# Linear attention, two mixtures and a cosine layer on one core: the tail's keys' products move into each step's sum

## The chip, the cores and the metric

One core of a Trainium2 chip runs the whole kernel. The metric is device microseconds of one execution. In profiled executions the profile also gives the span from the first to the last instruction.

## The reference

Attention with random features (a linear attention) is followed by two dense parts. Cut to what the change touches:

```python
# q, k, v: (2 batches, 8 heads, 576 tokens, 64);  omega: (128 features, 64)
def phi(x):
    proj = np.einsum('bhsd,md->bhsm', x, omega)
    h = proj - np.sum(x * x, axis=-1, keepdims=True) / 2.0
    h = h - np.max(h, axis=-1, keepdims=True)
    return np.exp(h) / np.sqrt(m)
q_p, k_p = phi(q * scale), phi(k * scale)
kv = np.einsum('bhsm,bhsd->bhmd', k_p, v)      # the keys' products: a sum over all 576 tokens
z = np.sum(k_p, axis=2)
num = np.einsum('bhsm,bhmd->bhsd', q_p, kv)
den = np.einsum('bhsm,bhm->bhs', q_p, z)[..., None] + 1e-06
x = num / den                                  # -> (1152 tokens, 512)
# then four experts: out += p[:, e:e+1] * (relu(x @ w1[e]) @ w2[e])
# then h = out @ w_in; result = (h * cos(h)) @ w_out
```

All arithmetic of the attention is in 32-bit floats.

## The kernel before

The 576 tokens of a batch are cut into 512 and a tail of 64. The 512 are worked on in eight pieces, one for each batch `b` and each pair of heads `hp`; in a piece a token is `4 * partition + r`, so each head has four groups `r` of 128 tokens. The tails of both batches stand together in one tile of 128 partitions, batch 0 in partitions 0 to 63, batch 1 in 64 to 127: `kL`, `qL`, `veL` (values, with a column of ones that gives the sum `z`), and `phiL`, the features of the tail's keys for all eight heads.

The attention is a loop over steps `s`, written out by hand, which sets the order of every engine's work. In a step TensorE makes, in this order: the numerators of the piece before last (`nums`, at the end of the step before), the keys' products of the last piece (`kv_of`), transposes of the next queries and keys (`turn_ahead`: `tp_q`, `tp_k`), transposes of the queries' features (`turn_phi`: `tq`), projections (`features`: `pj_q`, `pj_k`) and a transpose of the finished piece (`put_x`: `tx`). From step 6 on some products of the first expert (`dense_quanta`: `g`) stand between. After the loop come the dense parts, in an order of their own. A step's other engines: VectorE takes maxima of the projections, shifts, copies and divisions; ScalarE takes the exponentials and some copies; GpSimd sums squares.

The keys' products are in `kv_of(i)`. For each of the piece's two heads and each `r` the helper `column_halves` makes two products, one for each half of the 128 features, so that each uses 64 columns of the TensorE array and all 128 rows; the two stand in different columns. They are summed in PSUM over `r`. As the program's names go, the tile that is written is `kv` in the first step, and in later steps a free stretch of the bank that the numerators `num` of head 1 use (`room`), so in the profile `num<-ve,phk` is the keys' products too, and `num<-kv,pT` the numerators.

The tail's keys' products are made once, in step 1, by `kv_tail`: for each head, each half of the features and each batch one product of 64 rows and 64 columns, so that four neighbours use the four quarters of the array. They go to four banks (`kvL_z_b`), which VectorE copies to the tile `kvL`. In every step `kv_of` ends with a VectorE addition of the sum in PSUM and the part of `kvL` that belongs to it.

Of the kernel before, what the change touches and what calls it, by code (L numbers as in the profile page):

```python
# [9 lines left out]
F32 = mybir.dt.float32  # L10
F32R = mybir.dt.float32r
U32 = mybir.dt.uint32
ACTF = mybir.ActivationFunctionType
ALU = mybir.AluOpType
# [12 lines left out]
def performer_moe_kernel(ctx, tc, q, k, v, omega, probs, w1, w2, w_in, w_out, out):  # L27
    nc = tc.nc
    B, H, S, D = q.shape
    M = omega.shape[0]  # L30
# [31 lines left out]
    def bank(name):  # L62
        return ps.tile([P, 512], F32, tag="ps", name=name)
# [886 lines left out]
    with tc.tile_pool(name="at1", bufs=1) as at1, tc.tile_pool(name="at2", bufs=2) as at2:  # L950
# [102 lines left out]
        def features(nm, turned, phi, squares=None, shift_later=False):  # L1053

            nb = at2.tile([P, 2 * R], F32, tag=f"nb{nm}"[:3], name=f"nb_{nm}")
            pjs = [bank(f"pj_{nm}_{g}") for g in range(2)]
            for i in range(R):
                c = slice(i * P, (i + 1) * P)
                for z, (x_, y) in enumerate([(turned, ws)] + [(squares, minus_norm)] * (squares is not None)):
                    for g, pj in enumerate(pjs):  # L1060
                        r = slice(g * D, (g + 1) * D)
                        nc.tensor.matmul(  # L1062
                            pj[:, i * M : (i + 1) * M], x_[r, c], y[r, :],
                            start=z == 0, stop=z == (squares is not None),
                        )
            yield
            three = at2.tile([P, 2 * R, 3], F32, tag=f"th{nm[0]}", name=f"three_{nm}")
            def square_sum():
                nc.vector.tensor_reduce(out=three[:, :, 1], in_=sqs.pop(nm), op=ALU.add, axis=AX.X)

            if squares is None and nm != "q0":
                square_sum()
            for g, pj in enumerate(pjs):
                to = (nb if squares is not None else three[:, :, 0])[:, g : 2 * R : 2]
                nc.vector.tensor_reduce(
                    out=to, in_=pj.rearrange("p (a m) -> p a m", m=M), op=ALU.max, axis=AX.X,
                    negate=squares is not None,
                )
            if shift_later:
                yield  # L1080
            if squares is None:
                if nm == "q0":
                    square_sum()
                nc.vector.tensor_reduce(
                    out=three[:, :, 2], in_=three[:, :, 0:2], op=ALU.add, axis=AX.X, negate=True
                )
                nc.vector.tensor_reduce(out=nb, in_=three[:, :, 1:3], op=ALU.add, axis=AX.X)
            yield
            for g, pj in enumerate(pjs):
                for i in range(4):  # L1090
                    ix = g + 2 * i
                    nc.scalar.activation(
                        phi[:, ix, :], pj[:, i * M : (i + 1) * M], ACTF.Exp, bias=nb[:, ix : ix + 1]
                    )
                yield

        def divide(nm, parts):

# [36 lines left out]
        xss, phks, phqs, kts, qts = {}, {}, {}, {}, {}  # L1135

        kv = [at1.tile([P, 2, B, D + 1], F32, name=f"kv{hp}") for hp in range(NP)]
        kvL = at1.tile([P, H, B, D + 1], F32, name="kvL")

        def column_halves(dst, weights, moving, start=True, stop=True):  # L1140
            for z in range(2):
                c = slice(z * P // 2, (z + 1) * P // 2)
                nc.tensor.matmul(dst[c], weights[:, c], moving, start=start, stop=stop)  # L1143

        def kv_tail(phi):
            for z in range(2):
                hs = range(z * H // 2, (z + 1) * H // 2)
                sums_ = [
                    bank(f"kvL_{z}_{b}")[:, : H // 2 * (D + 1)].rearrange("p (h e) -> p h e", e=D + 1) for b in range(B)
                ]  # L1150
                for n, h in enumerate(hs):
                    for c in (slice(0, P // 2), slice(P // 2, P)):
                        for b in range(B):
                            bl = slice(b * L, (b + 1) * L)
                            nc.tensor.matmul(
                                sums_[b][c, n, :], phi[bl, h, c], veL[bl, h, :], start=True, stop=True
                            )
                for b in range(B):
                    nc.vector.tensor_copy(out=kvL[:, hs.start : hs.stop, b, :], in_=sums_[b])

        def kv_of(i):
            b, hp = pairs[i]
            ve, phk = ves[i % 2], phks.pop(i)
            kvp = room.pop() if room else bank(f"kv_{i}")
            kvp = kvp[:, 4 * (D + 1) : 6 * (D + 1)].rearrange("p (h e) -> p h e", h=2)
            for h in range(2):
                for r in range(R):
                    column_halves(
                        kvp[:, h, :], phk[:, h * R + r, :], ve[:, h * R + r, :], r == 0, r == R - 1
                    )  # L1170
            yield
            nc.vector.tensor_tensor(out=kv[hp][:, :, b, :], in0=kvp, in1=kvL[:, 2 * hp : 2 * hp + 2, b, :], op=ALU.add)

        pTs = {}
        room = []
# [173 lines left out]
        for s in range(NPR + 3):  # L1349
            if s == 0:  # L1350
                load_k(3)
                load_q(2)
                load_v(1)
            else:
                if s == 1:
                    advance(wload)
                if s > NPR:
                    dense_quanta(s, 2 * DQ)
                kvs = kv_of(s - 1) if s <= NPR else iter(())
                next(kvs, None)  # L1360
                if s == 1:
                    turn_phi(0)
                    kv_tail(phiL)
                    next(kvs, None)
                else:
                    turn_ahead(s)
                    if s < first:
                        advance(wload)
                    for _ in ks:
                        pass  # L1370
                    next(ns, None)
                    next(kvs, None)
                if s >= first:
                    advance(wload)
                if 2 <= s <= NPR:
                    turn_phi(s - 1)
                elif s == NPR + 1:
                    tail_turn_phi()
                px = iter(())
                if 2 <= s <= NPR + 1:  # L1380
                    b, hp = pairs[s - 2]
                    px = put_x(f"{s - 2}", hp, xss.pop(s - 2), b * R, R)
                qs = q_features(s) if s <= NPR else iter(())
                ks = k_features(s + 1, s < first) if s + 1 < NPR else iter(())
                next(qs, None)
                next(ks, None)
                next(px, None)
                next(px, None)
                next(qs, None)
                next(ks, None)  # L1390
                for _ in px:
                    pass
                dense_quanta(s, (2 if s > NPR else 4) * DQ)
                for _ in qs:
                    pass
                if s + 1 <= NPR:
                    norms_ahead(f"q{s + 1}", q_of(s + 1))
                if s + 2 < NPR:
                    norms_ahead(f"k{s + 2}", kts[s + 2])
                if s <= NPR:  # L1400
                    ns = nums(s - 1)
                    next(ns)
                elif s == NPR + 1:
                    tail_nums()
                else:
                    for _ in tail_put_x():
                        pass
                if s + 3 < NPR:
                    load_k(s + 3)
                if s + 2 < NPR:  # L1410
                    load_q(s + 2)
                if s + 1 < NPR:
                    load_v(s + 1)
            advance(wload)
            for kind, u in fetched.get(s, ()):
                wload.append(load_a(0, u, "p") if kind == "p" else load_v2(0, u))
                next(wload[-1])
            if s == 2:
                nc.vector.tensor_reduce(out=psum_, in_=pr, op=ALU.add, axis=AX.X)
            if s == 4:  # L1420
                nc.scalar.activation(psum_, psum_, ACTF.Copy, bias=1e-9)
            if s == first:
                nc.vector.reciprocal(out=psum_, in_=psum_)
                nc.vector.tensor_tensor(
                    out=pn, in0=pr, in1=psum_.to_broadcast([P, NTILE, E]), op=ALU.mult
                )
# [39 lines left out]
```

## Time and profile before

| | us |
|---|---|
| median of 3 runs (640.3 to 640.7) | 640.69 |
| profiled execution | 640.93 |
| its span | 639.2 |
| TensorE busy | 633.7 (99% of the span) |
| VectorE busy | 488.5 (76%) |
| ScalarE busy | 352.8 (55%) |
| GpSimd busy | 173.8 (27%) |

TensorE's granted clock is 1.00, that is 2.4 GHz, over the span. A matmul's end is modelled in the profile, so that its busy time covers short waits; what TensorE really spends is read from the starts of successive rows. A product in 32-bit floats leaves two records, so sixteen products are `x32`; a transpose leaves one.

### The profile page before, as it was taken

Reading aid. Unit: us, or ns where it says so; the run is one execution under the profiler, and the core shown is the slowest. Engines: PE = TensorE matmul, PEld = TensorE weight load, DVE = VectorE, ACT = ScalarE, POOL = GpSimd, SP = SyncE. Lnnn points to the kernel's source line nnn. Section 1 sums busy time; section 2 is a strip of 40 time slices with the busy share of each in tenths; the row PEclk is TensorE's granted clock in tenths of the full one; section 3 lists DMA queues with packets and bytes.
Section 4 is the critical chain, followed back from the end, with each engine's and each line's share of the span. In section 5 each row is a group of like instructions: output and inputs, shape, how many; then the busy total and the mean of one; then the engine's idle time right before and its main releaser. Section 6 shows DMA issues by size and latency. Waiting matters only on the chain.

```text
span 639.2 us, 10046 instructions
## 1 busy us (share of the span) xinstructions
PE 633.7 (99%) x3751; PEld 538.0 (84%) x3751; DVE 488.5 (76%) x878; ACT 352.8 (55%) x686; POOL 173.8 (27%) x218
## 2 busy tenths in 40 slices
PE   8999999999999999999999999999999999999997
PEld 7999989988888888888888888888888888888887
DVE  5998578789688688598687697699698772697842
ACT  6898664365346454354443455544457973476821
POOL 7899752033332333323333232310000000000000
PEclk9999999999999999999999999999999999999999
DMA  7645430313446434347424445401250002500111
GB/s 166 188 118 149 133 100 31 102 67 131 133 148 200 146 106 143 128 148 217 134 98 132 138 130 209 132 35 70 85 208 33 2 0 91 239 1 2 49 50 49
DMA packets 55440, 70.95 MB, mean 111 GB/s; under 512 B 15200, under 2 KB 40032, under 8 KB 55392
## 3 DMA queue, kind: packets, MB, share of 16 engines
q1 hardware_dynamic: 46800, 40.92, 20.5%
q0 software_dynamic: 8448, 29.37, 13.5%
q8 instruction: 29, 0.48, 0.3%
q14 instruction: 19, 0.16, 0.1%
q10 hardware_dynamic: 144, 0.03, 0.0%
HBM read 55.36 MB, written 14.94 MB: 110 GB/s over the span
## 4 chain that ended last, share of the span: by engine, by line
PE 97%; DVE 1%; DMA 1%; SPq 0%; issue 0%; DVEq 0%
PE g L779 46%; PE g_odd L585 4%; PE g L549 3%; PE g_1c L549 2%; PE g_0a L549 2%; PE g_3a L549 2%; PE g_2a L549 2%; PE g_1a L549 2%; PE g_3c L549 2%; PE g_2c L549 2%; PE g_0c L549 2%; PE num L1143 2%; PE pj_q L1062 1%; PE g_0d L549 1%; PE g_0b L549 1%; PE g_3e L549 1%
## 5 line engine op out<-in xcount | busy, mean ns | idle before, releaser
L749 ACT ACTIVATE sth<-h 128x512 fp32r<-128x512 f32 (+1 forms) x111 | 60.3, 555 | 80.3 <-PE g L779 66.4
L258 POOL TENSOR_TENSOR c<-c 128x512 uint32<-128x512 uint32 x32 | 46.9, 1467 | 84.6 <-issue 34.2
L752 DVE SCALAR_TENSOR_TENSOR stl<-h,sth 128x512 fp32r<-128x512 f32 (+1 forms) x72 | 48.9, 694 | 27.1 <-ACT sth L749 26.9
L779 PE MATMUL g<-v3h,sth 128*128 128x512 f32 (+1 forms) x110 | 42.9, 390 | 0.0
L779 PE MATMUL g<-v0h,sth 128*128 128x512 f32 (+1 forms) x110 | 42.7, 388 | 0.0
L779 PE MATMUL g<-v1h,sth 128*128 128x512 f32 (+1 forms) x110 | 42.7, 388 | 0.0
L779 PE MATMUL g<-v2h,stl 128*128 128x512 f32 (+1 forms) x110 | 42.5, 387 | 0.0
L779 PE MATMUL g<-v2h,sth 128*128 128x512 f32 (+1 forms) x110 | 42.5, 386 | 0.0
L779 PE MATMUL g<-v0h,stl 128*128 128x512 f32 (+1 forms) x110 | 42.4, 386 | 0.0
L779 PE MATMUL g<-v3l,sth 128*128 128x512 f32 (+1 forms) x110 | 42.4, 386 | 0.0
L779 PE MATMUL g<-v3h,stl 128*128 128x512 f32 (+1 forms) x110 | 42.4, 386 | 0.0
L779 PE MATMUL g<-v1h,stl 128*128 128x512 f32 (+1 forms) x110 | 42.4, 385 | 0.0
L779 PE MATMUL g<-v1l,sth 128*128 128x512 f32 (+1 forms) x110 | 42.4, 385 | 0.0
L779 PE MATMUL g<-v0l,sth 128*128 128x512 f32 (+1 forms) x110 | 42.4, 385 | 0.0
L779 PE MATMUL g<-v2l,sth 128*128 128x512 f32 (+1 forms) x110 | 42.4, 385 | 0.0
L293 DVE TENSOR_TENSOR stl<-h,sth 128x512 fp32r<-128x512 f32 (+1 forms) x39 | 22.8, 594 | 19.3 <-ACT sth L749 19.1
L451 DVE SCALAR_TENSOR_TENSOR c<-c 128x512 f32<-128x512 f32 (+1 forms) x38 | 25.0, 662 | 11.9 <-ACT c L449 11.7
L448 ACT ACTIVATE c<-h 128x512 f32<-128x512 f32 x32 | 19.9, 621 | 19.8 <-DVE h L626 19.8
L805 DVE SCALAR_TENSOR_TENSOR acc<-g,pn,acc 128x512 f32<-128x512 f32 x27 | 20.1, 745 | 6.7 <-PE g L779 6.7
L779 PEld LDWEIGHTS g<-v2h,stl 128*128 128x128 f32 x110 | 20.7, 188 | 4.5 <-DVE stl L752 0.4
L779 PEld LDWEIGHTS g<-v0h,stl 128*128 128x128 f32 x110 | 20.7, 188 | 4.3 <-DVE stl L752 0.2
L779 PEld LDWEIGHTS g<-v3h,stl 128*128 128x128 f32 x110 | 20.7, 188 | 4.2
(427 smaller groups left out, 1880.5 us busy)
## 6 DMA issues: line engine op xcount, KB each, us to landing
rv<-in_moe_w_dram SPq DMA_DIRECT2D x16, 512.0 KB, 3.9
c<-in_moe_w_in_dram POOLq DMA_DIRECT2D x16, 512.0 KB, 4.1
c<-in_moe_w_out_dram POOLq DMA_DIRECT2D x16, 512.0 KB, 3.9
kt<-in_k_dram SPq DMA_DIRECT2D x8, 256.0 KB, 3.5
qt<-in_q_dram SPq DMA_DIRECT2D x8, 256.0 KB, 4.0
ve<-in_v_dram SPq DMA_DIRECT2D x16, 128.0 KB, 4.0
ra_2as<-in_moe_w_dram SPq DMA_DIRECT2D x8, 256.0 KB, 3.3
out_dram<-acc SPq DMA_DIRECT2D x7, 256.0 KB, 2.3
```

What stands on the lines that cost most here:

```text
L258: nc.gpsimd.tensor_tensor(out=total, in0=t, in1=lw, op=ALU.add)
L293: nc.vector.tensor_tensor(out=dst, in0=x, in1=y, op=ALU.subtract)
L448: nc.scalar.activation(vv, src, ACTF.Copy, bias=0.25, scale=INV_2PI)
L451: nc.vector.scalar_tensor_tensor(out=vv, in0=kk, scalar=ROUND, in1=vv, op0=ALU.subtract, op1=ALU.subtract)
L549: nc.tensor.matmul(dst, x[:, o], y[:, kk], start=start and n == 0, stop=stop and n == 3 * kn - 1, skip_group_check=reopen,)
L585: nc.tensor.matmul(g, x[:, kk], w[:, :, :, kk, :], start=n == 0, stop=n == 3 * KD - 1)
L749: nc.scalar.activation(hi, src, ACTF.Relu if self.e < E else ACTF.Copy)
L752: nc.vector.scalar_tensor_tensor(out=to, in0=src, scalar=0.0, in1=hi.bitcast(F32), op0=ALU.max, op1=ALU.subtract)
L779: nc.tensor.matmul(g, x, y[:, o : o + w], start=n == 0, stop=n == 3 * FT - 1)
L805: nc.vector.scalar_tensor_tensor(out=acc[t], in0=src, scalar=p_, in1=acc[t], op0=ALU.mult, op1=ALU.add)
L1062: nc.tensor.matmul(pj[:, i * M : (i + 1) * M], x_[r, c], y[r, :], start=z == 0, stop=z == (squares is not None),)
L1143: nc.tensor.matmul(dst[c], weights[:, c], moving, start=start, stop=stop)
```

## The change

`kv_tail`, its four banks, the tile `kvL` and the four copies go. In `kv_of` each head's sum gets one more pair of products behind its four: the two halves of the features again, from `phiL` and `veL`, in the 64 partitions of the piece's batch, so of 64 rows and 64 columns. The sum is stopped there, and VectorE's addition becomes a copy. Those are as many products of the tail as before (32), four in each of eight steps. In `features` the eight exponentials of the tail's keys come in the order of heads 0, 1, 2, 4, 6, 3, 5, 7 in place of 0, 2, 4, 6, 1, 3, 5, 7. The others keep their order; the generator loses yields behind the exponentials that no caller relied on.

```diff
-            for g, pj in enumerate(pjs):
-                for i in range(4):
-                    ix = g + 2 * i
-                    nc.scalar.activation(
-                        phi[:, ix, :], pj[:, i * M : (i + 1) * M], ACTF.Exp, bias=nb[:, ix : ix + 1]
-                    )
-                yield
+            order = [g + 2 * i for g in range(2) for i in range(R)]
+            if squares is not None:
+                order.insert(1, order.pop(R))
+            for ix in order:
+                i, g = divmod(ix, 2)
+                nc.scalar.activation(
+                    phi[:, ix, :], pjs[g][:, i * M : (i + 1) * M], ACTF.Exp, bias=nb[:, ix : ix + 1]
+                )
...
-        def kv_tail(phi):
-            for z in range(2):
-                hs = range(z * H // 2, (z + 1) * H // 2)
-                sums_ = [
-                    bank(f"kvL_{z}_{b}")[:, : H // 2 * (D + 1)].rearrange("p (h e) -> p h e", e=D + 1) for b in range(B)
-                ]
-                for n, h in enumerate(hs):
-                    for c in (slice(0, P // 2), slice(P // 2, P)):
-                        for b in range(B):
-                            bl = slice(b * L, (b + 1) * L)
-                            nc.tensor.matmul(
-                                sums_[b][c, n, :], phi[bl, h, c], veL[bl, h, :], start=True, stop=True
-                            )
-                for b in range(B):
-                    nc.vector.tensor_copy(out=kvL[:, hs.start : hs.stop, b, :], in_=sums_[b])
...
+            bl = slice(b * L, (b + 1) * L)
             for h in range(2):
+                n = 2 * hp + h
                 for r in range(R):
-                    column_halves(
-                        kvp[:, h, :], phk[:, h * R + r, :], ve[:, h * R + r, :], r == 0, r == R - 1
-                    )
-            yield
-            nc.vector.tensor_tensor(out=kv[hp][:, :, b, :], in0=kvp, in1=kvL[:, 2 * hp : 2 * hp + 2, b, :], op=ALU.add)
+                    column_halves(kvp[:, h, :], phk[:, h * R + r, :], ve[:, h * R + r, :], r == 0, False)
+                column_halves(kvp[:, h, :], phiL[bl, n, :], veL[bl, n, :], False, True)
+            yield
+            nc.vector.tensor_copy(out=kv[hp][:, :, b, :], in_=kvp)
...
                 if s == 1:
                     turn_phi(0)
-                    kv_tail(phiL)
                     next(kvs, None)
```

TensorE's order in step 1 of the kernel before, from the first piece's keys' products to the next queries' projections; `kvL_0` and `kvL_1` are the banks of the two batches, and the last pair of lines of `kvL` repeats fifteen more times:

```order
L1143 MATMUL kv_359<-ve_131,phk_205 64x65 x16
L1182 MATMUL tq_0_376<-ident,phq_247 128x128 x4
L1182 MATMUL tq_1_383<-ident,phq_247 128x128 x4
L1155 MATMUL kvL_0_390<-veL,phiL 64x65
L1155 MATMUL kvL_1_391<-veL,phiL 64x65
```

The same place in the changed kernel, and the first row of what follows:

```order
L1142 MATMUL kv_358<-ve_131,phk_204 64x65 x8
L1142 MATMUL kv_358<-veL,phiL 64x65 x2
L1142 MATMUL kv_358<-ve_131,phk_204 64x65 x8
L1142 MATMUL kv_358<-veL,phiL 64x65 x2
L1166 MATMUL tq_0_379<-ident,phq_246 128x128 x4
L1166 MATMUL tq_1_386<-ident,phq_246 128x128 x4
L1062 MATMUL pj_q_0_397<-ws,xT_q_306 128x128
```

The 32 products between the transposes and the projections are gone, and two of them stand behind each head's eight. The shape printed is that of the output, 64 features by 65 columns; the rows of the array in use are 128 for `phk` and 64 for `phiL`.

TensorE's order in step 2, from the numerators of the first piece to the next transposes, as it is in each later step too; the lines with a minus are of before, those with a plus of the changed kernel:

```order
-L1143 MATMUL num_1_484<-kv_138,pT_1_388 64x65 x8
-L1143 MATMUL num_0_493<-kv_138,pT_0_381 64x65 x8
-L1143 MATMUL num_1_484<-ve_132,phk_311 64x65 x16
+L1142 MATMUL num_1_447<-kv_138,pT_1_391 64x65 x8
+L1142 MATMUL num_0_456<-kv_138,pT_0_384 64x65 x8
+L1142 MATMUL num_1_447<-ve_132,phk_310 64x65 x8
+L1142 MATMUL num_1_447<-veL,phiL 64x65 x2
+L1142 MATMUL num_1_447<-ve_132,phk_310 64x65 x8
+L1142 MATMUL num_1_447<-veL,phiL 64x65 x2
```

A run of sixteen products of one shape has become four runs of two shapes in turn.

VectorE's order in step 1, from the copies of the queries' features to the sum of the first piece, before (minus) and changed (plus):

```order
-L1187 COPY pT_1_388<-tq_1_383 128x512
-L1159 COPY kvL<-kvL_0_390 128x4x65
-L1159 COPY kvL<-kvL_1_391 128x4x65
-L1159 COPY kvL<-kvL_0_410 128x4x65
-L1159 COPY kvL<-kvL_1_411 128x4x65
-L1172 TENSOR_TENSOR kv_138<-kv_359,kvL 128x2x65
+L1171 COPY pT_1_391<-tq_1_386 128x512
+L1156 COPY kv_138<-kv_358 128x2x65
```

Four copies are gone, and the addition has become a copy in the same place.

## Rows read from the trace of the kernel before

**Rows 1.** The page: the span, and busy time by engine.

```profile
span 639.2 us, 10046 instructions
...
PE 633.7 (99%) x3751; PEld 538.0 (84%) x3751; DVE 488.5 (76%) x878; ACT 352.8 (55%) x686; POOL 173.8 (27%) x218
```

**Rows 2.** Waits of TensorE over the span: the longest of the three listed.

```profile
PE warm L958 <- DVE one L965: 1.0, 1, 1.0
```

**Rows 3.** Two steps: length, busy time of each engine, clock, DMA share, GB/s.

```profile
20.60:27.27 6.67, 6.67 (x122) 5.98 (x120) 6.31 (x22) 6.00 (x21) 6.02 (x9) 1.00 0.46 116
...
40.78:47.61 6.83, 6.83 (x123) 6.25 (x121) 6.59 (x22) 6.80 (x23) 6.35 (x9) 1.00 0.02 4
```

**Rows 4.** TensorE in order of time, steps 1 and 2: start, length, tile, count.

```profile
13.86 1.15 PE L1143 MATMUL kv<-ve,phk 128*64 128x65 f32 x32
14.95 1.09 PE L1182 MATMUL tq<-ident,phq 128*128 128x128 f32 x8
15.97 1.58 PE L1155 MATMUL kvL<-veL,phiL 64*64 64x65 f32 x64
17.50 1.16 PE L1062 MATMUL pj_q<-ws,xT_q 64*128 64x128 f32 x16
...
19.62 1.15 PE L1143 MATMUL num<-kv,pT 128*64 128x65 f32 x32
20.60 1.10 PE L1143 MATMUL num<-ve,phk 128*64 128x65 f32 x32
21.63 0.66 PE L1035 MATMUL tp_q<-ident,qt 128*128 128x128 f32 x4
...
22.56 1.18 PE L1182 MATMUL tq<-ident,phq 128*128 128x128 f32 x8
23.68 1.16 PE L1062 MATMUL pj_q<-ws,xT_q 64*128 64x128 f32 x16
```

**Rows 5.** Line 1143: duration of one record, least, median and greatest ns.

```profile
L1143 PE MATMUL num<-kv,pT x256: 222/222/271, 19.6 to 77.2; 128*64 128x65 f32 x128
```

**Rows 6.** TensorE in order of time: a block with other modes on both sides, end of step 8.

```profile
76.31 1.15 PE L1143 MATMUL num<-kv,pT 128*64 128x65 f32 x32
77.40 0.45 PE L549 MATMUL g<-xh,w1h 128*128 128x384 f32 x1
```

**Rows 7.** TensorE in order of time: projections of the tail's keys, and of step 8.

```profile
10.09 0.39 PE L1062 MATMUL pj_kL<-minus_norm,x2L 64*128 64x128 f32 x4
10.31 0.39 PE L1062 MATMUL pj_kL<-ws,xkL 64*128 64x128 f32 x4
...
69.34 1.19 PE L1182 MATMUL tq<-ident,phq 128*128 128x128 f32 x8
70.46 1.16 PE L1062 MATMUL pj_q<-ws,xT_q 64*128 64x128 f32 x16
71.55 0.66 PE L1116 MATMUL tx<-ident,xs 128*128 128x128 f32 x4
```

**Rows 8.** TensorE in order of time, parts of steps 5 and 6.

```profile
42.74 1.04 PE L1182 MATMUL tq<-ident,phq 128*128 128x128 f32 x8
43.71 1.16 PE L1062 MATMUL pj_q<-ws,xT_q 64*128 64x128 f32 x16
...
46.48 1.29 PE L1143 MATMUL num<-kv,pT 128*64 128x65 f32 x32
47.61 1.10 PE L1143 MATMUL num<-ve,phk 128*64 128x65 f32 x32
```

**Rows 9.** ScalarE in order of time: the exponentials of the tail's keys.

```profile
14.06 2.22 ACT L1092 ACTIVATE phiL<-pj_kL,nb_kL 128x128 f32<-128x128 f32 x8
```

**Rows 10.** SyncE's queue: issues of the tail's values; and their landing.

```profile
6.52 2.00 SPq L978 DMA_DIRECT2D veL<-in_v_dram  x2
...
DMA to landing us min/median/max: 5.2/5.4/5.5
```

**Rows 11.** VectorE in order of time, step 1: the copies of `kvL`.

```profile
17.32 1.43 DVE L1159 COPY kvL<-kvL 128x260 f32<-128x260 f32 x4
```

More of the change, by code (lines that the diff above doesn't have):

```diff
@@ L1137, in performer_moe_kernel @@
         kv = [at1.tile([P, 2, B, D + 1], F32, name=f"kv{hp}") for hp in range(NP)]
-        kvL = at1.tile([P, H, B, D + 1], F32, name="kvL")
         def column_halves(dst, weights, moving, start=True, stop=True):
```

## The prediction

> **What bounds the kernel now.** The page says that TensorE is busy for 99% of the span and no other engine for more than 76% [rows 1]. Since a busy TensorE can hide short waits, I looked next at its waits: three are listed, the longest 1.0 us, all ahead of the first piece and none in the loop over steps [rows 2]. The busy time by step shows the attention's balance: a step is 6.67 to 6.83 us long, with VectorE at 6.31 and 6.59 and ScalarE at 6.00 and 6.80 of it [rows 3]. So the other engines are close behind TensorE, but it has no listed idle time, and what TensorE does more or less in a step should move the step's end. From there on I read TensorE's own order of time, start to start.
>
> **The price of a product pair.** In step 1 the keys' products are 32 records in a row of 1.15 us [rows 4]; one record lasts 0.222 us [rows 5], so the last starts 1.15 - 0.22 = 0.93 us after the first. The next keys' products, 32 records in 1.10 us, need 0.88 us from first to last start. They differ in what stands ahead of them: those of step 1 follow products of 64 rows by 128 columns, those of step 2 follow numerators that use the same 128 rows by 64 columns. Where nothing changes, 31 intervals take 0.88 us, two halves start nearly together, and 32 records are 0.88 + 0.06 = 0.94 us. A pair of column halves (4 records) is then 0.117 us.
>
> **The price of a change of shape.** The first products after another shape cost 0.93 - 0.88 = 0.05 us more. Behind the last start, 13.86 + 0.93 = 14.79, the transposes begin at 14.95, so 0.16 us later in place of 0.06: 0.10 us more. A change costs 0.15 us on this reckoning. A check from other rows: numerators and keys' products back to back take 21.63 - 19.62 = 2.01 us for 64 records [rows 4], a block alone between other shapes 77.40 - 76.31 = 1.09 us for 32 [rows 6]; twice the second less the first leaves 0.17 us. Does it also hold where only the rows in use change, as 128 by 64 to 64 by 64 does? No row has that pair. The nearest is 64 by 128 and 128 by 128. Four records of a long run of projections are 10.31 - 10.09 = 0.22 us apart, so sixteen stream in 0.89 us, and the block alone between transposes takes 71.55 - 70.46 = 1.09 us: 0.20 us for the change [rows 7]. So a change of the rows alone costs too. The bounds for one new change are 0.10 (only what stands behind the last start) and 0.20 us; I take 0.15, the price of 64-column weights.
>
> The Trainium skill, TensorEngine Tiling (Array Packing), section Key Properties, says that changing the tiling mode, and not merely the tile, drains TensorE. By that rule the pair that no row shows costs as the others do, and the sum is the one below. The same section says that different tiles can load weights and multiply in parallel; if 128 by 64 and 64 by 64 counted as tiles of one mode, the sum would be that of the second rival. The trace agrees with the first sentence at every change of shape that it has.
>
> **What is added.** In each of eight steps, two pairs: 16 x 0.117 = 1.87 us. Before, a step's keys' products were entered and left once. Now the array goes from 64 columns with 128 rows to 64 rows, back, again to 64 rows, and from there to the transposes: three changes more per step, 24 x 0.15 = 3.60 us. Together 5.47 us, or 0.68 us a step.
>
> **What is removed.** The products of `kvL` and the changes around them stand between 15.97 and 17.50: 1.53 us [rows 4]. For as many products this is less than is added, since four of them shared the array and they were one block. The transposes ahead and the projections behind stay and meet each other, a change that other steps have.
>
> **What is hidden.** VectorE loses four copies, 1.43 us [rows 11], and its addition becomes a copy; both lie beside TensorE's order, and if TensorE's time were not the limit, they would be the gain of the third rival. The tail's values are issued at 6.52, the two issues taking 2.00 us, and land within 5.5 us, so by 14.0 [rows 10]; the first tail pair comes after eight products, at about 13.86 + 0.05 + 0.47 + 0.10 = 14.5. The tail's exponentials begin at 14.06 and take 2.22 us for eight, 0.28 each [rows 9], so that of head 0 is done at about 14.4 or a little later and, in the new order, that of head 1 some 0.28 us behind it, ahead of its use near 15.2. If the first is a little late, TensorE waits 0.05 us, which I count; the transposes, projections and VectorE's copies queue behind it. In the old order head 1 would have been fifth, at 15.5, and cost 0.2 us more. Nothing is added to any DMA queue.
>
> **What is given back.** TensorE has short waits that the list does not show. The same transposes take 1.12 us at 22.56 [rows 4] and 0.97 at 42.74; numerators take 0.98 us at 19.62 and 1.13 at 46.48 [rows 8]. I compared each stretch of steps 2 to 8 with the shortest of its kind: twelve exceed it, from the transposes at 22.56 to those at 69.34 [rows 7], 1.2 us in all. These are waits for ScalarE and VectorE, which a slower TensorE reaches later. Without its waits a step is about 6.5 us of TensorE; with 0.68 more it is 7.2, above VectorE's 6.3 to 6.6 and ScalarE's 6.0 to 6.8. I take 1.0 of the 1.2 us as absorbed; the bounds are 0 and 1.2.
>
> **Sum.** 5.47 + 0.05 - 1.53 - 1.0 = +3.0 us on the profiled execution's 640.93 (its span of 639.2 and 1.7 around it): 643.9. The median of the runs is 0.24 us lower, so 643.7 us. The later parts only begin later: their order is the same and TensorE is as full there. With a change at 0.10 us and all waits absorbed it would be 642.3, with 0.20 us 644.9 and with none absorbed 644.7; likeliest case by itself: 642.3 to 645.1.
>
> **Rivals.** First, that leaving or entering the 64-row shape costs more than any change seen here, or that the sum's reading of old values waits on what was just written: 0.1 us on each of 16 pairs is +1.6 us, 645.3. For it stands only that the trace has no such pair of shapes in one sum; against it, that products of one sum follow at 0.06 us. Second, that 128 by 64 and 64 by 64 do not count as a change: 1.87 + 0.05 - 1.53, less some 0.3 of absorbed waits, is +0.1, so 640.8 and the same. Against it stands that each change of shape in the trace has its price, also of rows alone. Third, on the other side: the step's pace is set by VectorE and ScalarE, TensorE's short waits are what shows of it, and the added products fall into that slack, while step 1 loses the 1.43 us of copies at the head of VectorE's chain. Then the kernel gains about 1.5 us, 639.2. It decides only if a step has room for what is added; the rows leave a step of 6.67 us some 0.19 us, against 0.68, or 0.23 without any price of a change.
>
> **How the numbers follow.** The likeliest case has 0.76, the first rival 0.06, the second 0.13, the third 0.05. A measurement of this kernel can tell about 0.2%, 1.3 us, from no change, so the first two are slower, 0.82; same 0.13; faster 0.05. The range reaches from the second rival, 640.6, to the top of the likeliest case, 645.1.
>
> **What would show it.** The stretch from the first record of the keys' products to the next transposes, 21.63 - 20.60 = 1.03 us in step 2, should be near 1.7 us in each step, with a gap of about 0.16 us at each turn between 128 and 64 rows. The rows of `kvL` should be gone and the projections of step 1 should start about 0.8 us earlier than 17.50, with the steps after 7.2 us long, and transposes of queries' features near 0.97 us. If the gaps stay at 0.06 us, the price of a change is wrong; if the steps stay at 6.7 us with those gaps, TensorE was not the pace; if a wait for the tail's exponentials or values stands in step 1, the order of arrival is.

## The result, and the profile after

| | before | changed |
|---|---|---|
| median of 5 runs, us | 640.70 (640.3 to 640.88) | 644.11 (643.54 to 644.67) |
| profiled execution | 640.93 | 644.11 |
| ratio | | 1.0053 [1.0039, 1.0067] |

The changed kernel is 3.4 us slower; 643.7 was forecast. The page of the changed kernel first, the span and busy time by engine:

```profile
span 642.3 us, 10038 instructions
...
PE 637.4 (99%) x3751; PEld 540.9 (84%) x3751; DVE 487.1 (76%) x874; ACT 353.4 (55%) x686; POOL 174.3 (27%) x218
```

TensorE still has 99%, and the same number of products. Beside [rows 1] it is busy 3.7 us longer, VectorE 1.4 us less: the four copies. Where TensorE's time went is read from its order of time in steps 1 and 2 (start, length, operation, tiles, count of records, and in brackets a listed wait), which answers to [rows 4]:

```profile
13.26 0.69 PE L1142 MATMUL kv<-ve,phk 128*64 128x65 f32 x16
14.12 0.33 PE L1142 MATMUL kv<-veL,phiL 64*64 64x65 f32 x4 [0.18 <-ACT phiL L1094]
14.38 0.69 PE L1142 MATMUL kv<-ve,phk 128*64 128x65 f32 x16
14.99 0.33 PE L1142 MATMUL kv<-veL,phiL 64*64 64x65 f32 x4
15.26 1.09 PE L1166 MATMUL tq<-ident,phq 128*128 128x128 f32 x8
16.28 1.16 PE L1062 MATMUL pj_q<-ws,xT_q 64*128 64x128 f32 x16
...
19.25 0.64 PE L1142 MATMUL num<-ve,phk 128*64 128x65 f32 x16
19.82 0.33 PE L1142 MATMUL num<-veL,phiL 64*64 64x65 f32 x4
20.08 0.69 PE L1142 MATMUL num<-ve,phk 128*64 128x65 f32 x16
20.70 0.33 PE L1142 MATMUL num<-veL,phiL 64*64 64x65 f32 x4
20.96 0.66 PE L1035 MATMUL tp_q<-ident,qt 128*128 128x128 f32 x4
21.45 0.60 PE L1035 MATMUL tp_k<-ident,kt 128*128 128x128 f32 x4
21.89 1.04 PE L1166 MATMUL tq<-ident,phq 128*128 128x128 f32 x8
22.85 1.16 PE L1062 MATMUL pj_q<-ws,xT_q 64*128 64x128 f32 x16
```

In step 2 the keys' products, from their first record to the next transposes, take 20.96 - 19.25 = 1.71 us, against 1.03 before. Each of the seven later steps shows +0.66 to +0.68. A tail pair between two runs of 128 rows takes 20.08 - 19.82 = 0.26 us, that is 0.117 for the pair and 0.14 for the change. In step 1 the block takes 15.26 - 13.26 = 2.00 us against 14.95 - 13.86 = 1.09: +0.91, which is 0.68 and some 0.23 of waiting for the tail's exponentials. The wait stands in the first sixteen records: 14.12 - 13.26 = 0.86 us, against 14.99 - 14.38 = 0.61 where nothing is awaited. The list of the products' waits gives only 0.18 of it, that of the weight loads 0.31.

So 7 x 0.68 + 0.91 = 5.67 us came in. From the transposes of step 1 to the projections it is now 16.28 - 15.26 = 1.02 us, in place of 17.50 - 14.95 = 2.55: 1.53 us went out. Net +4.14. By step, the two stretches of [rows 3] again (columns as there), from the keys' products of one step to those of the next:

```profile
19.25:26.58 7.33, 7.33 (x130) 6.50 (x128) 6.13 (x21) 6.22 (x21) 6.60 (x10) 1.00 0.52 149
41.35:48.86 7.51, 7.51 (x131) 6.72 (x128) 6.60 (x22) 6.82 (x23) 6.94 (x10) 1.00 0.19 56
```

Both are longer by what the keys' products gained (7.33 for 6.67, 7.51 for 6.83), with VectorE's and ScalarE's busy time within 0.25 us of what it was. Over the whole attention I compare from the first keys' product to the first product of the second dense layer's line 779, since in single executions the keys' products begin anywhere from 12.7 to 14.0 us (in the kernel before, 0.5 us of it is a wait for the load of `kL`). Before, that product starts at 84.20, after, here:

```profile
87.23 0.50 PE L779 MATMUL g<-v0h,sth 128*128 128x512 f32 x1
```

The stretch went from 84.20 - 13.86 = 70.34 to 87.23 - 13.26 = 73.97 us, +3.63, so 4.14 - 3.63 = 0.5 us was absorbed by waits that had been there. From there to the end of the span it is 555.0 and 555.1 us: the later parts only begin later.

Some of the short waits are gone, others not. The transposes of features at 21.89 take 0.96 us, the least of their kind; before, in the same step, 1.12 [rows 4]. But the numerators of steps 4 and 5 still start 1.13 us ahead of what follows, as in [rows 8], where 0.98 needs no wait. In TensorE's order of time:

```profile
40.22 1.30 PE L1142 MATMUL num<-kv,pT 128*64 128x65 f32 x32
41.35 0.64 PE L1142 MATMUL num<-ve,phk 128*64 128x65 f32 x16
```

### The profile page after: what moved, and what is told of

It reads as the page before. It is cut to its first block, busy times and chain, and to the rows that moved or that the text cites. A ratio compares the mean times of both kernels' runs of the same rounds, so it can differ in the third digit from the quotient of the medians.

```text
span 642.3 us, 10038 instructions
## 1 busy us (share of the span) xinstructions
PE 637.4 (99%) x3751; PEld 540.9 (84%) x3751; DVE 487.1 (76%) x874; ACT 353.4 (55%) x686; POOL 174.3 (27%) x218
## 4 chain that ended last, share of the span: by engine, by line
PE 95%; DVE 2%; ACT 1%; DMA 0%; issue 0%; DVEq 0%
PE g L779 44%; PE g_odd L585 4%; PE num L1142 3%; PE g L549 3%; PE g_1c L549 2%; PE g_0a L549 2%; PE g_3a L549 2%; PE g_2a L549 2%; PE g_1a L549 2%; PE g_2c L549 2%; PE g_3c L549 2%; PE g_0c L549 2%; PE pj_q L1062 1%; PE g_0d L549 1%; PE g_0b L549 1%; PE g_3e L549 1%
## 5 line engine op out<-in xcount | busy, mean ns | idle before, releaser
L779 PEld LDWEIGHTS g<-v1h,stl 128*128 128x128 f32 x110 | 20.7, 188 | 4.2
```

The source lines that it names most:

```text
L779: nc.tensor.matmul(g, x, y[:, o : o + w], start=n == 0, stop=n == 3 * FT - 1)
```

## The experiments

Each set was run beside the kernel before on the same chip; ratios are to it. The stretch is the one defined above, read from one execution each. It takes in a few tenths that belong to the execution: the waits for ScalarE's exponentials in step 1 differ from one to the next.

**1. The tail's products with all 128 rows.** `veL` is kept once for each batch, with zeros in the other batch's partitions, so that the sum is the same and the shape of the products does not change. Against the changed kernel:

```diff
-        veL = at1.tile([P, H, D + 1], F32, name="veL")
+        veL = [at1.tile([P, H, D + 1], F32, name=f"veL{b}") for b in range(B)]
+        for b in range(B):
+            nc.vector.memset(veL[b][(1 - b) * L : (2 - b) * L], 0.0)
...
-                column_halves(kvp[:, h, :], phiL[bl, n, :], veL[bl, n, :], False, True)
+                column_halves(kvp[:, h, :], phiL[:, n, :], veL[b][:, n, :], False, True)
```

> The changed kernel with the tail's pairs made over all 128 rows: the values of each batch's tail stand in a tile of their own with zeros in the other batch's 64 partitions, so that the same 16 pairs stand in the same places and no change between 128 and 64 rows is left. First theory (each of the 24 added changes of shape costs some 0.15 us): 3.5 us less than the changed kernel's 644.1, so 640.6, perhaps 0.3 more if waits come back; the keys' products up to the next transposes take about 1.27 us in place of 1.71. Rival (the pairs themselves are dear, because a sum that is still open is read and written again in other rows, or because TensorE's order is longer for other reasons): it stays within 1 us of 644.1.

641.25 us (640.27 to 641.94), ratio 1.0006 [0.9997, 1.0015]. The keys' products of step 2, in TensorE's order of time:

```profile
19.27 0.64 PE L1144 MATMUL num<-ve,phk 128*64 128x65 f32 x16
19.73 0.29 PE L1144 MATMUL num<-veL,phiL 128*64 128x65 f32 x4
19.85 0.64 PE L1144 MATMUL num<-ve,phk 128*64 128x65 f32 x16
20.32 0.29 PE L1144 MATMUL num<-veL,phiL 128*64 128x65 f32 x4
20.54 0.66 PE L1037 MATMUL tp_q<-ident,qt 128*128 128x128 f32 x4
```

A tail pair now takes 19.85 - 19.73 = 0.12 us and the block 1.27. The same products without their three changes of shape are 1.71 - 1.27 = 0.44 us a step cheaper, 0.147 for each change; seven steps make 3.1 us, and step 1 gains 0.3, since it waits 0.1 us longer for `phiL` here. The stretch is 3.4 us shorter (70.60) and the time 2.9 us less. The price of a change of rows alone is thereby shown; the time is 0.65 us above the 640.6 that was forecast. Of the 0.5 us between the stretch and the time, 0.3 is that this execution began its keys' products later (13.58 for 13.26). Behind the stretch 0.25 us came back: TensorE's list of waits has a new one there, 0.34 us for VectorE's tile `stl` at 99.33 us.

**2. The two tail pairs of a step side by side.** Head 0's pair stays behind its eight products, head 1's pair goes ahead of its own, so that a step has one run of 64 rows where it had two:

```diff
+                if h == 1:
+                    column_halves(kvp[:, h, :], phiL[bl, n, :], veL[bl, n, :], True, False)
...
+                if h == 0:
+                    column_halves(kvp[:, h, :], phiL[bl, n, :], veL[bl, n, :], False, True)
```

> The changed kernel with head 1's tail pair ahead of its four others, right behind head 0's: two changes of shape more per step than in the kernel before, in place of three. First theory: 8 changes fewer, 8 x 0.15 = 1.2 us less than the changed kernel, 642.9, and 1.56 us in place of 1.71 from the first keys' product to the next transposes. Rival (the price belongs to each tail pair, not to the change of shape): no difference, 644.1.

642.67 us (642.42 to 643.06), ratio 1.0032 [1.0019, 1.0044]. Step 2 in TensorE's order of time:

```profile
18.85 0.64 PE L1142 MATMUL num<-ve,phk 128*64 128x65 f32 x16
19.41 0.45 PE L1142 MATMUL num<-veL,phiL 64*64 64x65 f32 x8
19.80 0.69 PE L1142 MATMUL num<-ve,phk 128*64 128x65 f32 x16
20.41 0.66 PE L1035 MATMUL tp_q<-ident,qt 128*128 128x128 f32 x4
```

The block is 1.56 us, 0.15 less than 1.71, for one change less; eight steps should give 1.2 us, and the time fell by 1.4. The cost goes with the number of changes, not with that of products.

**3. The removed part alone.** The kernel before without `kv_tail` and with a copy for the addition. It leaves the tail's tokens out of the sums over the keys.

```diff
-            nc.vector.tensor_tensor(out=kv[hp][:, :, b, :], in0=kvp, in1=kvL[:, 2 * hp : 2 * hp + 2, b, :], op=ALU.add)
+            nc.vector.tensor_copy(out=kv[hp][:, :, b, :], in_=kvp)
...
-                    kv_tail(phiL)
```

> The kernel before without the tail's keys' products: this one leaves the tail's tokens out of the sums over keys; the VectorE addition is a copy. It shows what the removal alone is worth. First theory: TensorE's block of 1.53 us goes from its order, 639.2, and at most 0.3 us more from shorter waits behind it. Rival (step 1 is paced by VectorE, whose four copies hide the block or are hidden by it): 640.7 if the block was hidden, or under 638.5 if VectorE's chain set the pace of the steps behind.

640.63 us (640.23 to 640.79), ratio 0.9997 [0.9988, 1.0005]: taking 1.53 us from TensorE is worth nothing that shows, and by the interval at most 0.8 us. The time is the rival's, but not its mechanism, since step 1 did get shorter: from its transposes to its projections it takes 1.13 us in place of 2.55. TensorE's order of time shows where the time came back, first in step 2:

```profile
20.19 1.40 PE L1181 MATMUL tq<-ident,phq 128*128 128x128 f32 x8
21.52 1.16 PE L1062 MATMUL pj_q<-ws,xT_q 64*128 64x128 f32 x16
22.71 1.16 PE L1062 MATMUL pj_k<-ws,xT_k 64*128 64x128 f32 x16
...
60.58 0.66 PE L1116 MATMUL tx<-ident,xs 128*128 128x128 f32 x4 [0.28 <-ACT phk L1092]
...
98.79 0.50 PE L779 MATMUL g<-v2h,stl 128*128 128x512 f32 x1 [0.57 <-DVE stl L752]
```

The transposes that stream in 0.97 us take 21.52 - 20.19 = 1.33, and the projections behind them 1.19 for 1.00. The list of the products' waits has neither; that of the weight loads (PEld) has both, 0.38 and 0.22 us, for ScalarE's exponentials. The first of them:

```profile
20.93 0.42 PEld L1181 LDWEIGHTS tq<-ident,phq 128*128 128x128 f32 x4 [0.38 <-ACT phq L1092]
```

Those exponentials (18.71 to 20.88 us) had themselves waited 1.00 us for VectorE's `nb_q`, and VectorE has no listed wait in its order of time from 13 to 18.6 us. In step 2, then, VectorE's work and ScalarE's behind it hold TensorE up. Over the stretch only 0.44 of the 1.53 us is left (69.90 for 70.34), and behind it that is lost too (556.0 us to the end, for 555.0), to waits such as the last row's. TensorE is not alone at the limit. Of GpSimd I looked at the step near 60 us. This is the same row in the kernel before, the changed one and this one:

```profile
61.07 1.27 POOL L134 TENSOR_TENSOR w3l<-ra_3p,w3h 128x512 fp32r<-128x512 f32 x1 [0.46 <-ACT w3h L129]
```
```profile
63.00 1.27 POOL L134 TENSOR_TENSOR w3l<-ra_3p,w3h 128x512 fp32r<-128x512 f32 x1 [2.02 <-ACT w3h L129]
```
```profile
60.40 2.54 POOL L134 TENSOR_TENSOR w3l<-ra_3p,w3h 128x512 fp32r<-128x512 f32 x2
```

GpSimd's work waits 0.46 us for the others before, 2.02 in the changed kernel, and not at all here. That alone does not show that GpSimd holds TensorE up. The kernel of experiment 6 below has the same work as the kernel before up to this row, but in its profiled execution the keys' products began at 12.80 us, not 13.86, and it has no wait here either:

```profile
60.56 2.53 POOL L134 TENSOR_TENSOR w3l<-ra_3p,w3h 128x512 fp32r<-128x512 f32 x2
```

The kernel of experiment 3 began them at 13.05 us. So the 0.46 us is no fixed reserve, and experiment 5 has to decide.

**4. The changed kernel with the old order of the tail's exponentials.**

```diff
-            if squares is not None:
-                order.insert(1, order.pop(R))
```

> The changed kernel with the tail's exponentials in the old order, so head 1 is the fifth. Only the wait in step 1 is looked at. If the wait of about 0.25 us in the changed kernel is for head 0's exponential, it stays, and a second one of 0.1 to 0.2 us appears ahead of head 1's pair; the first projections of step 1 start that much later. If it is for the tail's values, there is one wait as before. The time moves by less than can be measured.

643.86 us in a single execution. Step 1, TensorE's order of time:

```profile
13.33 0.69 PE L1140 MATMUL kv<-ve,phk 128*64 128x65 f32 x16
14.01 0.33 PE L1140 MATMUL kv<-veL,phiL 64*64 64x65 f32 x4
14.27 0.69 PE L1140 MATMUL kv<-ve,phk 128*64 128x65 f32 x16
15.04 0.33 PE L1140 MATMUL kv<-veL,phiL 64*64 64x65 f32 x4
```

The two runs of sixteen take 0.68 and 0.77 us where 0.61 needs no wait: 0.07 and 0.16 us, 0.23 in all, about what the new order has at head 0 alone. In this execution the exponentials began 0.20 us behind the first product (13.53), in the changed kernel's 0.31 (13.57 for 13.26), so that up to 0.1 us in favour of the new order isn't excluded. The 0.2 that was forecast is not seen.

**5 and 6. GpSimd relieved.** If GpSimd's chain holds the kernel of experiment 3 up, taking work from it should bring part of the 1.53 us out. The splits of the first four blocks of second weights go to VectorE, once in the kernel of experiment 3 (which still leaves the tail out) and once in the kernel before:

```diff
-        yield from split(nc.gpsimd if e == 0 else nc.vector, raw, *units["v", e, u])
+        yield from split(nc.vector, raw, *units["v", e, u])
```

> The kernel without the tail's keys' products (it leaves the tail's tokens out of the sums over keys) and with the low parts of the first expert's second weights (v0 to v3) made by VectorE in place of GpSimd. Theory formed on the run without the tail: there TensorE ran into a chain that does not depend on it, GpSimd's work one piece behind the other, with the weight buffers that it gives back, the loads that wait for them and ScalarE's work queued behind those loads. With 10 us taken from GpSimd in this stretch, part of the 1.5 us comes out: about 639.6, and the waits near 60, 82 and 99 us shrink. Rival (the removal comes to nothing because of ScalarE's and VectorE's own work in steps 2 to 5): 640.6 as without the relief, or slower, since VectorE has 5 us more.

> The kernel before with v0 to v3's low parts made by VectorE. First theory: TensorE's own order is just above GpSimd's chain in the kernel before, so little is to be had: 640.2 to 640.7. Rival (the chain already costs the kernel before about as much as a faster TensorE would bring): under 640.

Without the tail: 639.75 us (639.55 to 639.91), ratio 0.9983 [0.9974, 0.9992], 0.9 us below experiment 3 by the ratios. In the kernel before: 640.49 (640.23 to 641.29), ratio 0.9994 [0.9985, 1.0002], not told from no change. So the same relief is worth 0.9 us where TensorE has less to do, by intervals that just tell it from nothing, and not a measurable amount where it has its old work; the two amounts are not told from each other. Without the tail, the waits behind the stretch are gone from TensorE's list, which now reads (engine, line, waited for: us, times, longest):

```profile
PE warm L958 <- DVE one L965: 1.0, 1, 1.0
PE tx L1116 <- ACT phk L1092: 0.4, 1, 0.4
PE num L1142 <- DVE pT L1186: 0.3, 1, 0.3
```

The waits in step 2 and near 60 us stayed, and one for VectorE, which has the splits now, is new. GpSimd's splits are part of the floor; in step 2 it is VectorE and ScalarE, as shown above. In the kernel of experiment 6 the stretch is 71.11 us, 0.8 more than before with the same work of TensorE: 0.3 of it in step 1, in a wait for ScalarE, and most of the rest around step 8, in waits for VectorE.

**7 and 8. Added work at two places.** To see what the kernel before absorbs, six pairs of products with zeros, of the neighbours' own shape, go into each of the eight steps: behind the keys' products (7), or ahead of the numerators of head 1 (8). They write to a free stretch of the bank that nothing reads.

```diff
+            for _ in range(6):
+                column_halves(spare_, zero, zero[:, : D + 1])
```

> The kernel before with six more pairs of products in each of the eight steps, zeros into unused columns of the bank, 128 rows by 64 columns as the others, right behind the keys' products: 8 x 6 x 0.117 = 5.6 us of TensorE and no change of shape. Theory on what is given back: waits at the end of a step are those of VectorE's and ScalarE's work that begins with the transposes behind the keys' products, so time put ahead of those transposes delays that work too, and little is absorbed: 0.5 us, 645.8. Rival (a slower step absorbs most of the 1.2 us of waits wherever the time is put): 645.1 or less.

> The same six pairs a step, put ahead of the numerators, at the end of a step and so behind the transposes and projections on which VectorE and ScalarE work. Theory on what is given back: these do absorb, the waits ahead of and in the numerators and at the next projections: about 1.1 us, 645.2, and 0.5 us or more below the run with the pairs behind the keys' products; the numerators' wait of 0.15 us in steps 4 and 5 is gone. Rival (place does not matter): the two runs within 0.3 us of each other.

Six pairs are 0.70 us, in eight steps 5.6. Behind the keys' products the kernel takes 646.23 us (645.91 to 647.12), ratio 1.0085 [1.0071, 1.0099], and the stretch is 76.04, +5.7: on balance nothing is absorbed, where 0.5 us was forecast. Ahead of the numerators it takes 645.63 (645.02 to 645.94), ratio 1.0072 [1.0058, 1.0086], and the stretch is 75.38, +5.0: 0.57 us is absorbed, where 1.1 was forecast. The intervals of the two ratios overlap, so that the times alone do not tell the two places apart. TensorE's order of time at the same step does, with the work behind the keys' products:

```profile
42.40 1.30 PE L1143 MATMUL num<-kv,pT 128*64 128x65 f32 x32
43.52 1.10 PE L1143 MATMUL num<-ve,phk 128*64 128x65 f32 x32
44.46 0.87 PE L1143 MATMUL num<-zero 128*64 128x65 f32 x24
```

and with it ahead of the numerators:

```profile
41.77 0.92 PE L1143 MATMUL num<-zero 128*64 128x65 f32 x24
42.52 1.10 PE L1143 MATMUL num<-kv,pT 128*64 128x65 f32 x32
43.46 1.10 PE L1143 MATMUL num<-ve,phk 128*64 128x65 f32 x32
```

In the first the numerators still take 43.52 - 42.40 = 1.12 us; in the second 0.94, the length without a wait and without a change of shape. Steps 4 and 5 together make 0.3 us of the 0.66 by which the stretches differ. Most of the rest is two waits that only the kernel of experiment 7 has: 0.3 us at the projections of step 1 and 0.2 at a product of the first expert at 79.55 us.

**9. Experiment 1 with GpSimd's relief.** Both edits together, to see whether 128 rows without the wait near 99 us beats the kernel before.

> The tail's pairs inside each step over all 128 rows, as in the first experiment, and v0 to v3's low parts made by VectorE. The first experiment had a wait of 0.5 us near 99 us that the kernel before does not have; if that is GpSimd's chain, it goes, and the kernel comes to 640.3 to 640.8, level with the kernel before. Rival (the wait there belongs to the tail's pairs): 641.2 as in the first experiment.

640.66 us (640.35 to 641.38), ratio 0.9998 [0.9989, 1.0007]. The wait near 99 us is gone, and the kernel is level with the one before. No version ran measurably faster than that with the whole computation in it.

## Why the prediction came out as it did

**Price of a change: right.** 0.15 us forecast, 0.147 by experiment 1 and 0.15 by experiment 2; the block of 1.7 us stands in every step after the first. The second rival (128 rows by 64 columns and 64 by 64 as one mode) would have left the block near 1.27 us. It is 1.71, and experiment 1 shows 1.27 when the rows really stay. The Trainium skill, TensorEngine Tiling (Array Packing), section Key Properties, has that a change of tiling mode drains TensorE; the runs agree in that each change has a price, also where only the rows change, and put 0.15 us beside it. That it is a drain no run here shows. The first rival (a dearer 64-row shape, 0.1 us a pair more) would have given 0.88 a step; it is 0.68.

**Added work: right but for step 1.** 5.47 us forecast without waits; the steps have 8 x 0.68 = 5.44. The wait for `phiL` was mis-sized: 0.05 us forecast, about 0.23 measured, and some 0.37 in experiments 1 and 9. And the old order of exponentials was said to cost 0.2 us more; experiment 4 shows 0.23 us in all with it. Part of the miss is the single execution: the forecast rested on exponentials that begin 14.06 - 13.86 = 0.20 us behind the first product, and here it is 13.57 - 13.26 = 0.31.

**Removed work: right as a time of TensorE, 1.53 us, but not as a gain of its own.** This is what the forecast's reasons lacked. It took TensorE as the only pace, with 1.2 us of waits above it, and passed over GpSimd, which has 6.02 and 6.35 us in the same [rows 3]. Experiment 3 shows that below the old total other engines hold the kernel: 1.53 us less gives 0.9997. Above it the added time shows nearly in full, as experiment 7 has it. The parts therefore don't add up one by one; the sum held because the net change was well above zero. Counted from the kernel of experiment 3, the addition brings the stretch from 69.90 to 73.97, 4.07 of its 5.67 us, since the first 1.6 us of it falls into the waits that the removal had opened.

**Waits absorbed: mis-sized.** 1.0 us forecast, 0.5 measured. The step that failed is "these are waits for ScalarE and VectorE, which a slower TensorE reaches later". Compared row by row, the twelve waits, 1.2 us in all, fall into three kinds:

- The transposes of features (1.12 us in steps 2 and 8) are back at 0.97, and two waits of the queries' projections are gone or halved. That is about the 0.5 us absorbed. The transposes wait for exponentials of projections that stand in the step before, ahead of the added products, so a slower TensorE does reach them later.
- The numerators of steps 4 and 5 kept their 0.3 us.
- The projections of the keys in steps 3 to 6, counted as 0.4 us of waits by the shortest of their kind, are as long as before in the changed kernel and in experiments 7 and 8. What they wait for, if for anything, is open.

So that step holds only for time added behind what the producers themselves wait for. The numerators' second half needs ScalarE's copy `pT`, which ends 0.55 us behind the numerators' start in both kernels (40.21 for 39.66, 40.79 for 40.22). Ahead of that copy ScalarE has that of `tp_k` and a row of exponentials, and a step of VectorE begins with the copy of `tp_q`. Those transposes stand right behind the keys' products, so that the longer block delays both engines as much as TensorE. Their lists of waits over 12 to 82 us have, VectorE before and then after:

```profile
DVE xT_q L1046 <- PE tp_q L1035: 2.6, 2, 2.4
```
```profile
DVE xT_q L1046 <- PE tp_q L1035: 8.4, 7, 3.6
```

and ScalarE after, where it had none of this kind before:

```profile
ACT xT_k L1044 <- PE tp_k L1035: 3.6, 5, 0.8
```

Experiments 7 and 8 test it with work of one size at two places: the numerators' waits stay with the work ahead of `tp_q` and go with it behind. Their sums over the stretch, 0 and 0.57 us, show it less purely, since in the kernel of experiment 7 the waits of the transposes went as well and two others came. The two mis-sizings, 0.2 and 0.5 us, both lengthened the stretch: +3.6 us in place of +3.0. The medians differ by 3.4, and the two profiled executions by 3.2, since that of before happened to begin its keys' products 0.6 us later.

**The third rival, on the other side, fell in its main claim.** A step had no room for 0.68 us. But its premise, that other engines set a pace close under TensorE's, is what experiment 3 shows, and it should have changed the working of the removed part.

**The range.** The bottom of the likeliest case is worked out, its top of 645.1 is not: with 0.20 us a change and no wait absorbed the sum gives 645.9. The result does not touch it.

What stays open is how the floor divides among GpSimd, ScalarE and VectorE in steps 3 to 5, and what a relief of VectorE or ScalarE would bring: the waits there stayed when GpSimd was relieved of later work, and no run took work from the others.

## What to carry to other kernels

Group small products by the shape that they use of the array, or pad them to their neighbours' shape: a pair with half its rows zero cost 0.12 us, the same pair in its own 64 rows between two others 0.26. Of an engine that is busy for 99%, time added and time removed are to be judged apart: 5.6 us more showed in full here, 1.53 us less did not show. Look first at how closely the other engines' chains follow, in more than one execution: one such wait was 0.46 us in one and gone in another with the same work up to there. And a wait absorbs added work only if that work does not stand ahead of what the producer that is waited for itself waits for.

## What was not expected of the hardware

Products of 64 rows and of 128 rows sum into one place in PSUM, one right behind the other, with no price beyond the change of shape (0.14 to 0.15 us). And short waits are drawn as busy time of the products: the transposes of experiment 3 as 1.40 us, though 0.97 us is all that they need. The list of the products' waits has nothing of it; that of the weight loads has 0.38 us, but not the 0.15 us inside the numerators of steps 4 and 5.
